# Clustered attention and two MLPs on one core: another order for the comparisons, the weight conversion and the output tiles

## The chip, the cores and the metric

One core of one Trainium2 chip runs the whole program. The metric is the device time of one execution in microseconds (us). TensorE is called PE here (PEld is its weight load), VectorE DVE, ScalarE ACT, GpSimd POOL, and SP is the engine that issues most of the DMAs. A number like L503 is a line of the kernel before.

## What is computed

The inputs q, k and v have the shape (2, 8, 768, 64) in float32; there are 16 centroids for each of the 8 heads. Every query and every key goes to its nearest centroid, and a query sees the keys of its own cluster only:

```python
q_assign = np.argmax(np.einsum('bhsd,hcd->bhsc', q_n, c_n), axis=-1)
k_assign = np.argmax(np.einsum('bhsd,hcd->bhsc', k_n, c_n), axis=-1)
mask = q_assign[:, :, :, None] == k_assign[:, :, None, :]
scores = np.where(mask, scale * q @ k.T, -1e9)
attn = exp(scores - max) / (sum + 1e-9);  x = attn @ v
```

The result, 1536 rows of 512, goes through two MLPs one after the other, each 512 → 2048 → 512. The first has g = h · cos h between its two products, the second g = h for h ≥ 1, 0 for h ≤ −1 and (h + 1)² / 4 between. The weights of both MLPs arrive as 64-bit floats.

## The kernel before, in words

**Attention.** The work is cut into 8 pairs (a batch entry and two heads), each with 4 units (a head, and one half of the queries): 32 units u. A unit has 6 slots k = 0 to 5. `run_slot` goes through all slots in order, and the order in which Python emits the instructions is the order of each engine's list: nothing is reordered behind it. Work for a later slot is queued by `later(n, f)` and emitted by `next_slot` n slots on.

In every slot, PE transposes a third of the unit's probabilities (`p_transpose`, L550), and ACT or, for k = 2 and 5, DVE copies them to SBUF (L555, L553). In slots 0, 2 and 5 PE also makes the scores of a tile of the next unit (L494, L497) into one of two PSUM buffers; DVE takes their row max (L503) and ACT the exp (L512), which frees the buffer. In slot 5 `p_v` (L564) multiplies with v, and ACT copies the output (`o_parts`, L575). PE's transposes all go through three PSUM buffers, `ps_t`, in turn, whoever uses them.

**The path to x.** Some slots after the exps DVE makes reciprocals of the row sums (L529) and POOL spreads them (`spread`, L536, tile rb). When both heads of a half are done, POOL moves rows together (`o_rows`, L584, L585), PE transposes rb into r and DVE multiplies (`finish`, L594, L596), and POOL splits the result into a high and a low part (`x_parts`, L601, L602: xh and xl, which the first MLP reads).

**Preparing a pair.** `prep_pair` is a generator, and `plan` says in which slot each of its eleven steps runs, and whether ahead of the unit's p_v (False) or behind everything else in the slot (True): four steps that transpose q and k (L332), the products with the centroids dt (L389) and their transposition pd (L396), the comparisons (L443 and L444 on DVE; L446 on POOL; L449; L451 on DVE), which end in one-hot rows (tile dots), and last the transposition of those (L468, tile po), the scaling on ACT (L470, oht) and eight copies by DMA (L477) into the stacked tiles st that the scores read. For pair i ≥ 2 the comparisons begin in slot 23 counted from the pair i − 2, the last slot of a unit, so one unit in four carries them: the units 3, 7, 11, 15, 19 and 23, six in all.

**Weight conversion.** The weights come in 32 chunks. `convert_chunk` has six steps, in turn: abs on ACT (L142); DVE L144; L146; L149; DVE L152 with the high part on POOL (L158) and the DMA of the next chunk; the low part on DVE (L161). A chunk's raw words and its working tile wx each have one buffer, so the six steps of a chunk follow each other. During the attention one step runs behind the last slot of each unit from the ninth on (`pump` and `CONVERT`, 24 steps); the others run in the MLPs.

**MLPs.** `hidden` makes four blocks h of 128 columns with 12 matmuls each (L724 to L726) into four PSUM buffers; `g_cosine` then runs on ACT (n, L697; sine and square, L699 and L700) and DVE (r, L698; g, L703), and `output` multiplies with the second weight. The first hidden block's matmuls are the first PE work behind the attention. A weight slot is written by the conversion and read by the matmuls.

**Pools.** All tiles of the attention, xt0, xt1, xt2 and rb among them, are in `apool`, which is given back behind the last unit; the MLP's pool `mpool`, with the tile n, takes the same bytes.

Of the kernel before, what the change touches and what calls it, by code (L numbers as in the profile page):

```python
# [31 lines left out]
def attention_moe_moe(  # L32
# [73 lines left out]
    def later(n, f, *args):  # L106
        due.setdefault(now[0] + n, []).append((f, args))
# [13 lines left out]

    w0pool = ctx.enter_context(tc.tile_pool(name="w0pool", bufs=1))
    wslot = []
    wchunks = []
# [68 lines left out]
    with ExitStack() as actx:  # L193
# [37 lines left out]
        def centroid_load():  # L231
            ct = ap.tile([P, HS], F32, tag="xt0", bufs=2, name="ct")[:, :P].rearrange(
                "p (r d) -> p r d", r=2)
            nc.scalar.dma_start(ct[:, 0], centroids.rearrange("h c d -> (h c) d"))
            return ct

        def centroid_setup(ct):
# [9 lines left out]
            for _ in range(2):  # L247
# [6 lines left out]
            nc.vector.reciprocal(ss[:, 3:4], ss[:, 2:3])  # L254
            cd = ap.tile([P, HS], F32, tag="xt1", bufs=2, name="cd")[:, :P].rearrange(
                "p (r d) -> p r d", r=2)
# [20 lines left out]
        def prep_pair(i):  # L277
# [84 lines left out]
            if i == 0:  # L362
                dcs = []
                for s in range(2):
                    dt = ps_t.tile([P, HS], F32, tag="t", name=f"dt0_{s}")
                    for hf in range(2):
                        g = hf * 2 * C
                        with tc.issue_after(ins(tr)):
                            nc.tensor.matmul(dt[g:g + 2 * C], cw, t32s[(s, hf)],
                                             start=True, stop=True, tile_position=(0, g))  # L370
                    dc = ap.tile([P, HJ, P], F32, tag=("oht", "xt2")[s], bufs=1 + s, name=f"dc0_{s}")
                    dc = dc[:4 * C]
                    if s == 0:
                        nc.vector.tensor_copy(dc.rearrange("p j n -> p (j n)"), dt[:4 * C])
                    else:
                        nc.scalar.activation(dc.rearrange("p j n -> p (j n)"), dt[:4 * C], AF.Copy)
                    dcs.append(dc)
# [154 lines left out]
        def spread(u, den):  # L532
            i, h, hf = units[u]
            if h == 0:
                rb[(i, hf)] = ap.tile([P, HJ, 2, D], F32, tag="rb", bufs=2, name=f"rb{i}_{hf}")
            nc.gpsimd.tensor_scalar(  # L536
                rb[(i, hf)][:, :, h], den[:, :, 1].unsqueeze(2).to_broadcast([P, HJ, D]),
                1.0, 0.0, ALU.mult, ALU.add)
# [28 lines left out]
        def o_parts(u):  # L567
# [4 lines left out]

            t = ap.tile([P, HS], F32, tag=f"xt{h}", bufs=2, name=f"xt{h}_{i}_{hf}")
            xt.setdefault((i, hf), []).append(t)
            nc.scalar.activation(t, o, AF.Copy)  # L575
            if h == 1:
                later(1 if i == len(pairs) - 1 else 3, o_rows, i, hf, main, other)

        def o_rows(i, hf, main, other):
            t0, t = xt[(i, hf)]  # L580
            t2 = ap.tile([P, HS], F32, tag="xt2", bufs=2, name=f"xt2_{i}_{hf}")
            xt[(i, hf)] = (t, t2)
            for dst, rows, src in ((t2, other, t0[main]), (t2, main, t[other]), (t, other, t0[other])):
                nc.gpsimd.tensor_scalar(dst[rows], src, 1.0, 0.0, ALU.mult, ALU.add)  # L584
            nc.gpsimd.tensor_tensor(t, t, t2, ALU.add)  # L585
            later(2 if i == len(pairs) - 1 else 4, finish, i, hf)

        def finish(i, hf):
# [7 lines left out]
            nc.vector.tensor_tensor(t2, t1, r, ALU.mult)  # L596
            later(1 if i == len(pairs) - 1 else 2, x_parts, hp, b * S + hf * HS, t2)

# [26 lines left out]

        def run_steps(slot, batch_done):
            for made in steps.pop((slot, batch_done), ()):
                next(made)

        plan(1, *((n, True) for n in (-6, -5, -4, -3, -2, -1, -1, 0, 1, 2, 3)))  # L630
        for i in range(2, len(pairs)):
            s0 = (i - 2) * PAIR
            plan(i, *((s0 + n, d) for n, d in (
                (5, True), (11, False), (11, True), (17, False), (17, True), (23, False),
                (23, True), (24, True), (26, True), (27, True), (29, False))))

        def run_slot(slot):
            u, k = divmod(slot, NJ)
            at_slots = (0, 2, 4) if u < 0 else (0, 2, 5)
            new = -1 <= u < len(units) - 1 and k in at_slots  # L640
            n = (u + 1) * HJ + at_slots.index(k) if new else None
# [4 lines left out]
            if new and k == 0:  # L646
                scores_of(n)
            if u >= 0:
                p_transpose(u, k)
            if new and k > 0:  # L650
                scores_of(n)
            run_steps(slot, False)
            if u >= 0 and k == NJ - 1:
                p_v(u)
            if new:
                row_max(n)
                if k == NJ - 1:
                    row_exp(n)
            elif -1 <= u < len(units) - 1 and k in [m + 1 for m in at_slots]:
                row_exp((u + 1) * HJ + at_slots.index(k - 1))  # L660
            if u >= 0 and k == NJ - 1:
                o_parts(u)
            next_slot()
            if slot == 47:
                issue_chunk(0)
            run_steps(slot, True)
            if slot in CONVERT:
                pump(1)

        CONVERT = [n * NJ + NJ - 1 for n in range(8, 32)]  # L670
        with tc.manual_schedule(engines={
# [142 lines left out]
```

## Time and profile before

| | |
|---|---|
| median of 3 runs | 800.97 us (800.7 to 803.86) |
| the profiled execution | 800.59 us, its span 798.5 us |
| busy share of the span | PE 97%, PEld 77%, DVE 71%, ACT 48%, POOL 34% |
| mean granted clock of PE | 0.995 of full speed |
| attention up to the first unit's p_v | 31.09 us |
| the stretch of units from there to 259.09 us | 228.00 us, PE busy for 220.65 |
| the last units and the first hidden block, to 283.24 us | 24.15 us, PE busy for 18.58 |
| the rest of both MLPs | 515.26 us, PE busy for 511.65 |

The span runs from the first to the last instruction; the time of an execution is some 2 us more. Busy is time in which an engine runs an instruction; the ends of matmuls are modelled, so a stretch is better measured from one start to another. In a timeline an idle time is noted behind the instruction that it precedes, with what ended it: `[1.92 <-PE r L594]` means that the engine stood for 1.92 us until PE had made r at L594.

### The profile page before, as it was taken

Reading aid. Unit: us, or ns where it says so; the run is one execution under the profiler, and the core shown is the slowest. Engines: PE = TensorE matmul, PEld = TensorE weight load, DVE = VectorE, ACT = ScalarE, POOL = GpSimd, SP = SyncE. Lnnn points to the kernel's source line nnn. Section 1 sums busy time; section 2 is a strip of 40 time slices with the busy share of each in tenths; the row PEclk is TensorE's granted clock in tenths of the full one; section 3 lists DMA queues with packets and bytes.
Section 4 is the critical chain, followed back from the end, with each engine's and each line's share of the span. In section 5 each row is a group of like instructions: output and inputs, shape, how many; then the busy total and the mean of one; then the engine's idle time right before and its main releaser. Section 6 shows DMA issues by size and latency. Waiting matters only on the chain.

```text
span 798.5 us, 10663 instructions
## 1 busy us (share of the span) xinstructions
PE 775.5 (97%) x3935; PEld 611.1 (77%) x3936; DVE 565.0 (71%) x809; ACT 384.1 (48%) x712; POOL 268.4 (34%) x398
## 2 busy tenths in 40 slices
PE   8899999999999889999999999999999999999998
PEld 4576776676677668888888888888888888888886
DVE  6565767666777498777887888788868887755552
ACT  6678777786787375443334344222444332222220
POOL 4346557666534632221221212342131222111110
PEclk9999999999999999999999999999999999999999
DMA  8755654755240212313112122111221311000012
GB/s 199 162 136 122 175 124 126 164 140 123 62 121 2 68 43 102 105 53 106 53 56 103 53 80 79 53 54 53 68 91 53 106 53 53 1 0 1 16 51 92
DMA packets 46387, 65.93 MB, mean 83 GB/s; under 512 B 27904, under 2 KB 30848, under 8 KB 46336
## 3 DMA queue, kind: packets, MB, share of 16 engines
q1 hardware_dynamic: 46192, 65.22, 28.8%
q8 instruction: 31, 0.51, 0.3%
q14 instruction: 20, 0.16, 0.1%
q10 hardware_dynamic: 144, 0.03, 0.0%
HBM read 43.02 MB, written 3.15 MB: 58 GB/s over the span
## 4 chain that ended last, share of the span: by engine, by line
PE 64%; POOL 1%; ACT 1%; DVE 0%; issue 0%; POOLq 0%
PE y L726 11%; PE y L724 11%; PE y L725 11%; PE h L724 10%; PE h L726 10%; PE h L725 10%; POOL xt L585 0%; POOL xh L601 0%; POOL xt L584 0%; ACT L699 0%; ACT r L699 0%; ACT n L697 0%; POOL xl L602 0%; DVE g L703 0%; DVE acc L763 0%; DVE xt L596 0%
## 5 line engine op out<-in xcount | busy, mean ns | idle before, releaser
L686 POOL TENSOR_SCALAR gh<-g 128x512 fp32r<-128x512 f32 x96 | 72.0, 750 | 276.6 <-DVE g L717 163.0
L724 PE MATMUL h<-xh,w 128*128 128x512 f32 x384 | 149.6, 390 | 3.4 <-DVE g L703 3.4
L725 PE MATMUL h<-xl,w 128*128 128x512 f32 x384 | 149.5, 389 | 0.0
L726 PE MATMUL h<-xh,w 128*128 128x512 f32 x384 | 149.5, 389 | 0.0
L503 DVE TENSOR_REDUCE nm<-s 128x1 f32<-128x768 f32 x96 | 91.6, 954 | 42.6 <-PE s L497 39.7
L512 ACT ACTIVATE p<-s,nm 128x768 f32<-128x768 f32 x96 | 86.8, 904 | 22.3 <-DVE nm L503 15.4
L713 ACT ACTIVATE p<-h,ones 128x512 f32<-128x512 f32 x48 | 33.1, 690 | 132.5 <-DVE m L712 132.1
L690 DVE TENSOR_TENSOR gl<-g,gh 128x512 fp32r<-128x512 f32 x96 | 73.6, 768 | 21.0 <-POOL gh L686 15.2
L724 PEld LDWEIGHTS h<-xh,w 128*128 128x128 f32 x384 | 72.1, 188 | 18.7 <-DVE g L703 3.8
L725 PEld LDWEIGHTS h<-xl,w 128*128 128x128 f32 x384 | 72.1, 188 | 14.9
L726 PEld LDWEIGHTS h<-xh,w 128*128 128x128 f32 x384 | 72.1, 188 | 14.9
L550 PE MATMUL pt<-ident,p 128*128 128x128 f32 x576 | 77.5, 275 | 4.4 <-DVE p_t L553 2.7
L142 ACT ACTIVATE wx<-wraw 128x1024 f32<-128x1024 f32 x32 | 36.3, 1135 | 86.5 <-DMA wraw<-in_moe_w_out_dram 39.0
L550 PEld LDWEIGHTS pt<-ident,p 128*128 128x128 f32 x576 | 66.9, 141 | 10.9 <-DVE p_t L553 4.6
L494 PE MATMUL s<-st,st 128*128 128x384 f32 x192 | 74.1, 386 | 0.8 <-ACT p L512 0.5
L724 PE MATMUL y<-gh,w 128*128 128x512 f32 x192 | 74.7, 389 | 0.0
L725 PE MATMUL y<-gl,w 128*128 128x512 f32 x192 | 74.7, 389 | 0.0
L726 PE MATMUL y<-gh,w 128*128 128x512 f32 x192 | 74.7, 389 | 0.0
L724 PE MATMUL y<-w,gh 128*128 128x512 f32 x192 | 74.7, 389 | 0.0
L725 PE MATMUL y<-w,gh 128*128 128x512 f32 x192 | 74.7, 389 | 0.0
L726 PE MATMUL y<-w,gl 128*128 128x512 f32 x192 | 74.7, 389 | 0.0
L763 DVE TENSOR_TENSOR acc<-y,acc 128x512 f32<-128x512 f32 x72 | 49.1, 684 | 33.9 <-PE y L726 33.9
(118 smaller groups left out, 1376.9 us busy)
## 6 DMA issues: line engine op xcount, KB each, us to landing
wraw<-in_moe_w_in_dram SPq DMA_DIRECT2D x16, 1024.0 KB, 5.1
wraw<-in_moe_w_out_dram SPq DMA_DIRECT2D x16, 1024.0 KB, 4.7
st<-t SPq DMA_DIRECT2D x24, 192.0 KB, 4.2
st<-th SPq DMA_DIRECT2D x9, 384.0 KB, 3.9
st<-tl SPq DMA_DIRECT2D x18, 192.0 KB, 4.1
st<-th SPq DMA_DIRECT2D x18, 192.0 KB, 4.2
nat<-in_q_dram SPq DMA_DIRECT2D x8, 384.0 KB, 4.9
nat<-in_k_dram SPq DMA_DIRECT2D x8, 384.0 KB, 5.1
```

The source lines that it names most:

```text
L142: nc.scalar.activation(x, high.bitcast(F32), AF.Abs)
L494: nc.tensor.matmul(s[:, step, :HS], qt[:, 0, cols], kt[:, 0, kc], start=True, stop=False)
L503: nc.vector.tensor_reduce(nm, s[:, :, :HS], AX.XY, ALU.max, negate=True)
L512: nc.scalar.activation(p, s[:, :, :HS], AF.Exp, bias=nm, accum_out=dens[u][:, jj, 0:1])
L550: nc.tensor.transpose(ps[:, jj * P:(jj + 1) * P], p[:, kt * P:(kt + 1) * P], ident)
L686: nc.gpsimd.tensor_scalar(hi, g, 1.0, 0.0, ALU.mult, ALU.add)
L690: nc.vector.tensor_tensor(lo, g, hi.bitcast(F32), ALU.subtract)
L713: nc.scalar.activation(r, ph, AF.Relu, bias=mone)
L724: nc.tensor.matmul(o, lh, rh, start=first, stop=False)
L725: nc.tensor.matmul(o, lh, rl, start=False, stop=False)
L726: nc.tensor.matmul(o, ll, rh, start=False, stop=last)
L763: nc.vector.tensor_tensor(a, po, a, ALU.add)
```

## The change

Five things change.

- The tiles xt0, xt1, xt2, rb, and those of the start that share their buffers, go to a pool of their own, `xpool`, opened early and never given back before the end.
- `plan` gets four places in a slot instead of two: ahead of the transposition, ahead of p_v, beside (behind the output's copy and ahead of `next_slot`, that is, ahead of what `later` queued) and behind. For pairs from the third on, L443 and L444 go from behind to beside in slot 23, L449 from behind to ahead of the row max in slot 26, L451 from slot 27 to slot 29 ahead of p_v, and the one-hot transposition L468 with what follows from ahead of p_v in slot 29 to behind it. The second pair's steps are planned later as well: dt from before the first unit's slots to its slot 0, the comparisons from there to slots 2 to 5, L468 to slot 6.
- The second exp of a unit moves from slot 3 to slot 4, behind the copy of that slot.
- The conversion starts with unit 15 and follows a pattern over four units: in each fourth unit (15, 19, ...) abs ahead of p_v and L144 beside; then L146; then L149 and L152 together; then L161. That is 26 steps up to the last unit.
- The counts of `later` change: `o_rows` 3 slots on for all but the last unit, `finish` always 4, `x_parts` always 1.

```diff
+    xpool = ctx.enter_context(tc.tile_pool(name="xpool", bufs=1))
...
-            ct = ap.tile([P, HS], F32, tag="xt0", bufs=2, name="ct")[:, :P].rearrange(
+            ct = xpool.tile([P, HS], F32, tag="xt0", bufs=2, name="ct")[:, :P].rearrange(
...
-                rb[(i, hf)] = ap.tile([P, HJ, 2, D], F32, tag="rb", bufs=2, name=f"rb{i}_{hf}")
+                rb[(i, hf)] = xpool.tile([P, HJ, 2, D], F32, tag="rb", bufs=2, name=f"rb{i}_{hf}")
...
-            t = ap.tile([P, HS], F32, tag=f"xt{h}", bufs=2, name=f"xt{h}_{i}_{hf}")
+            t = xpool.tile([P, HS], F32, tag=f"xt{h}", bufs=2, name=f"xt{h}_{i}_{hf}")
...
-                later(1 if i == len(pairs) - 1 else 3, o_rows, i, hf, main, other)
+                later(1 if u == len(units) - 1 else 3, o_rows, i, hf, main, other)
...
-            t2 = ap.tile([P, HS], F32, tag="xt2", bufs=2, name=f"xt2_{i}_{hf}")
+            t2 = xpool.tile([P, HS], F32, tag="xt2", bufs=2, name=f"xt2_{i}_{hf}")
...
-            later(2 if i == len(pairs) - 1 else 4, finish, i, hf)
+            later(4, finish, i, hf)
...
-            later(1 if i == len(pairs) - 1 else 2, x_parts, hp, b * S + hf * HS, t2)
+            later(1, x_parts, hp, b * S + hf * HS, t2)
...
-        plan(1, *((n, True) for n in (-6, -5, -4, -3, -2, -1, -1, 0, 1, 2, 3)))
+        AHEAD_OF_T, AHEAD_OF_V, BESIDE, BEHIND = range(4)
+        plan(1, (-6, BEHIND), (-5, BEHIND), (-4, BEHIND), (-3, BEHIND), (0, AHEAD_OF_T),
+             (2, BEHIND), (2, BEHIND), (3, BEHIND), (5, BESIDE), (5, BESIDE), (6, BEHIND))
         for i in range(2, len(pairs)):
             s0 = (i - 2) * PAIR
             plan(i, *((s0 + n, d) for n, d in (
-                (5, True), (11, False), (11, True), (17, False), (17, True), (23, False),
-                (23, True), (24, True), (26, True), (27, True), (29, False))))
+                (5, AHEAD_OF_V), (11, AHEAD_OF_V), (11, BEHIND), (17, AHEAD_OF_V), (17, BEHIND),
+                (23, AHEAD_OF_V), (23, BESIDE), (24, BEHIND), (26, AHEAD_OF_V),
+                (29, AHEAD_OF_V), (29, BEHIND))))
...
+            exp_slots = (1, 3, 5) if u < 0 else (1, 4)
...
+            run_steps(slot, AHEAD_OF_T)
             if u >= 0:
                 p_transpose(u, k)
             if new and k > 0:
                 scores_of(n)
-            run_steps(slot, False)
+            run_steps(slot, AHEAD_OF_V)
+            if u >= FIRST and k == NJ - 1 and u % 4 == 3:
+                pump(1)
             if u >= 0 and k == NJ - 1:
                 p_v(u)
...
-            elif -1 <= u < len(units) - 1 and k in [m + 1 for m in at_slots]:
-                row_exp((u + 1) * HJ + at_slots.index(k - 1))
+            elif -1 <= u < len(units) - 1 and k in exp_slots:
+                row_exp((u + 1) * HJ + exp_slots.index(k))
             if u >= 0 and k == NJ - 1:
                 o_parts(u)
+            run_steps(slot, BESIDE)
+            if u >= FIRST and k == NJ - 1:
+                pump((1, 2, 1, 1)[u % 4])
             next_slot()
             if slot == 47:
                 issue_chunk(0)
-            run_steps(slot, True)
-            if slot in CONVERT:
-                pump(1)
-
-        CONVERT = [n * NJ + NJ - 1 for n in range(8, 32)]
+            run_steps(slot, BEHIND)
+
+        FIRST = 15
```

DVE, around the end of unit 11, where the comparisons of the fifth pair (mx4, eq4, dots4) stand. s38 to s41 are tiles of scores and nm38 to nm41 their row maxima; p12_t2 and p12_t5 are copies of transposed probabilities; L596 multiplies with r. Before:

```order
L503 TENSOR_REDUCE nm38_1595<-s38_1579 128x1
L529 RECIPROCAL den11_1436<-den11_1436 128x3
L596 TENSOR_TENSOR xt2_2_0_1541<-xt1_2_0_1497,r2_0_1602 128x384
L443 TENSOR_REDUCE mx4_1607<-pd4_1584 128x24
L444 TENSOR_TENSOR eq4_1608<-pd4_1584,mx4_1607 128x384
L149 SCALAR_TENSOR_TENSOR wx0_1310<-wraw0_1185,wx0_1310 128x1024
L503 TENSOR_REDUCE nm39_1623<-s39_1612 128x1
L553 COPY p12_t2_1648<-pt12_2_1644 128x384
L503 TENSOR_REDUCE nm40_1655<-s40_1650 128x1
L449 TENSOR_REDUCE mx4_1607<-eq4_1608 128x24
L451 TENSOR_TENSOR dots4_1502<-eq4_1608,mx4_1607 128x384
L553 COPY p12_t5_1677<-pt12_5_1673 128x384
```

After:

```order
L504 TENSOR_REDUCE nm38_1594<-s38_1578 128x1
L444 TENSOR_REDUCE mx4_1600<-pd4_1583 128x24
L445 TENSOR_TENSOR eq4_1601<-pd4_1583,mx4_1600 128x384
L530 RECIPROCAL den11_1436<-den11_1436 128x3
L597 TENSOR_TENSOR xt2_2_0_1540<-xt1_2_0_1497,r2_0_1605 128x384
L504 TENSOR_REDUCE nm39_1621<-s39_1610 128x1
L554 COPY p12_t2_1646<-pt12_2_1642 128x384
L450 TENSOR_REDUCE mx4_1600<-eq4_1601 128x24
L504 TENSOR_REDUCE nm40_1654<-s40_1648 128x1
L554 COPY p12_t5_1674<-pt12_5_1670 128x384
L452 TENSOR_TENSOR dots4_1502<-eq4_1601,mx4_1600 128x384
L504 TENSOR_REDUCE nm41_1700<-s41_1676 128x1
```

L443 and L444 (L444 and L445 after) now stand ahead of the reciprocal and of L596; the conversion step L149 has left this place; L449 stands ahead of the row max nm40 and L451 behind the copy p12_t5, where before they stood one behind the other between the two.

POOL, the same place (rb2_1 is the spread of unit 11; xh and xl are the parts of x; the L584 rows move output rows together for the next half). Before:

```order
L536 TENSOR_SCALAR rb2_1_1426<-den11_1436 128x3x64
L446 TENSOR_TENSOR eq4_1608<-eq4_1608,desc_63 128x384
L584 TENSOR_SCALAR xt2_2_1_1637<-xt0_2_1_1396 64x384
L584 TENSOR_SCALAR xt2_2_1_1637<-xt1_2_1_1599 64x384
L584 TENSOR_SCALAR xt1_2_1_1599<-xt0_2_1_1396 64x384
L585 TENSOR_TENSOR xt1_2_1_1599<-xt1_2_1_1599,xt2_2_1_1637 128x384
L601 TENSOR_SCALAR xh_103<-xt2_2_0_1541 128x384
L602 TENSOR_TENSOR xl_104<-xt2_2_0_1541,xh_103 128x384
```

After:

```order
L537 TENSOR_SCALAR rb2_1_1426<-den11_1436 128x3x64
L602 TENSOR_SCALAR xh_103<-xt2_2_0_1540 128x384
L603 TENSOR_TENSOR xl_104<-xt2_2_0_1540,xh_103 128x384
L447 TENSOR_TENSOR eq4_1601<-eq4_1601,desc_63 128x384
L585 TENSOR_SCALAR xt2_2_1_1637<-xt0_2_1_1397 64x384
L585 TENSOR_SCALAR xt2_2_1_1637<-xt1_2_1_1598 64x384
L585 TENSOR_SCALAR xt1_2_1_1598<-xt0_2_1_1397 64x384
L586 TENSOR_TENSOR xt1_2_1_1598<-xt1_2_1_1598,xt2_2_1_1637 128x384
```

The parts of x for the first half, L601 and L602, stood behind the rows of the second half and now stand ahead of L446 (L447 after), which is ahead of those rows in both.

ACT, where the attention ends and the first MLP begins (p31_t3 and p31_t4 are copies for the last unit, wx4 is a chunk's abs, xt1_7_1 the last output's copy, n and r belong to the first hidden block), with the semaphores that each row waits for, named by the engine or DMA queue that sets them. Before:

```order
L555 ACTIVATE p31_t3_3519<-pt31_3_3515 128x384 [waits PE_49,Activation_49]
L555 ACTIVATE p31_t4_3525<-pt31_4_3521 128x384 [waits PE_49]
L142 ACTIVATE wx4_3776<-wraw4_3486 128x1024 [waits DMAHW0_49,DVE_49,Pool_49]
L575 ACTIVATE xt1_7_1_3540<-o31_3533 128x384 [waits PE_49]
L697 ACTIVATE n_0_0_0_0_3591<-h0_0_0_0_3578 128x512 [waits DMAHW2_49,DMAHW3_49,DMAHW1_49,DMAHW4_49,DVE_49,DMAHW5_49,PE_49,DMAHW6_49,Activation_49,Pool_49]
L697 ACTIVATE n_0_0_0_1_3613<-h0_0_0_1_3600 128x512 [waits PE_49]
L699 ACT_TABLE_LOAD
L699 ACTIVATE r_0_0_0_0_3592<-r_0_0_0_0_3592 128x512 [waits DVE_49]
```

After:

```order
L556 ACTIVATE p31_t3_3516<-pt31_3_3512 128x384 [waits PE_49,Activation_49]
L556 ACTIVATE p31_t4_3522<-pt31_4_3518 128x384 [waits PE_49]
L143 ACTIVATE wx4_3530<-wraw4_3406 128x1024 [waits DMAHW0_49,DVE_49]
L576 ACTIVATE xt1_7_1_3539<-o31_3532 128x384 [waits PE_49]
L706 ACTIVATE n_0_0_0_0_3597<-h0_0_0_0_3584 128x512 [waits DMAHW3_49,DMAHW2_49,DMAHW4_49,DMAHW1_49,DMAHW5_49,PE_49,DMAHW6_49,Activation_49,Pool_49]
L708 ACT_TABLE_LOAD
L708 ACTIVATE r_0_0_0_0_3598<-r_0_0_0_0_3598 128x512 [waits DVE_49]
L706 ACTIVATE n_0_0_0_1_3619<-h0_0_0_1_3606 128x512 [waits PE_49]
```

The first n (L697, L706 after) waited for DVE among the others and now doesn't; the sine of the first block now stands ahead of the second n.

## Rows read from the trace of the kernel before

**Rows 1.** The page, busy time, share of the span and number of instructions.
```profile
PE 775.5 (97%) x3935; PEld 611.1 (77%) x3936; DVE 565.0 (71%) x809; ACT 384.1 (48%) x712; POOL 268.4 (34%) x398
```

**Rows 2.** Windows: stretch, us, PE, PEld, DVE, ACT, POOL busy (instructions), clock, DMA share, GB/s.
```profile
28.88:32.29 3.41, 3.41 (x14) 2.30 (x14) 1.51 (x2) 1.05 (x3) 0.00 (x0) 0.50 0.00 0
53.82:62.18 8.36, 7.59 (x50) 5.35 (x49) 6.21 (x11) 5.70 (x14) 3.66 (x6) 1.00 0.11 24
114.35:123.75 9.40, 7.88 (x50) 5.34 (x49) 7.34 (x13) 5.45 (x13) 5.05 (x7) 1.00 0.34 89
131.35:138.35 7.00, 7.00 (x49) 5.41 (x48) 5.19 (x8) 5.85 (x15) 6.24 (x9) 1.00 0.52 165
145.86:154.73 8.87, 7.90 (x50) 5.34 (x49) 6.81 (x13) 5.45 (x13) 4.51 (x7) 1.00 0.43 110
176.58:186.01 9.43, 7.92 (x49) 5.34 (x48) 7.37 (x13) 5.44 (x13) 5.55 (x8) 0.99 0.78 205
186.01:195.09 9.08, 9.08 (x53) 6.25 (x52) 4.60 (x8) 6.62 (x14) 4.99 (x9) 0.82 0.67 148
283.24:798.50 515.26, 511.65 (x2256) 423.35 (x2256) 378.41 (x504) 183.17 (x285) 112.79 (x135) 1.00 0.17 60
```

**Rows 3.** Timeline of DVE: start, us, instruction, idle before; unit from 114.35, one later.
```profile
117.09 0.55 DVE L596 TENSOR_TENSOR xt<-xt,r 128x384 f32<-128x384 f32 x1 [1.92 <-PE r L594]
117.56 0.55 DVE L443 TENSOR_REDUCE mx<-pd 128x24 f32<-128x384 f32 x1
...
118.69 1.22 DVE L149 SCALAR_TENSOR_TENSOR wx<-wraw,wx 128x1024 int32<-128x1024 int32 x1
...
121.16 0.95 DVE L503 TENSOR_REDUCE nm<-s 128x1 f32<-128x768 f32 x1
...
134.74 0.96 DVE L503 TENSOR_REDUCE nm<-s 128x1 f32<-128x768 f32 x1 [1.45 <-PE s L497]
```

**Rows 4.** Timeline of PE, the two waits of the unit from 114.35.
```profile
121.29 0.55 PE L550 MATMUL pt<-ident,p 128*128 128x128 f32 x3 [0.78 <-DVE p_t L553]
...
123.30 0.52 PE L468 MATMUL po<-ident,dots 128*128 128x128 f32 x3 [0.42 <-DVE dots L451]
```

**Rows 5.** Timeline of PE, the start.
```profile
22.70 0.55 PE L396 MATMUL pd<-ident,dc 128*128 128x128 f32 x3 [0.58 <-ACT dc L392]
...
28.28 0.52 PE L468 MATMUL po<-ident,dots 128*128 128x128 f32 x3 [2.05 <-DVE dots L451]
```

**Rows 6.** Timeline of PE, the end of the attention and the first hidden block.
```profile
265.87 0.55 PE L594 MATMUL r<-ident,rb 128*128 128x128 f32 x3 [1.53 <-POOL rb L536]
...
270.87 0.55 PE L594 MATMUL r<-ident,rb 128*128 128x128 f32 x3 [0.64 <-POOL rb L536]
...
279.45 0.39 PE L726 MATMUL h<-xh,w 128*128 128x512 f32 x1
283.24 0.50 PE L724 MATMUL h<-xh,w 128*128 128x512 f32 x1 [3.41 <-DVE g L703]
```

**Rows 7.** Timeline of ACT, the same place.
```profile
278.40 1.09 ACT L697 ACTIVATE n<-h 128x512 int32<-128x512 f32 x2 [6.80 <-POOL xl L602]
```

**Rows 8.** Groups of instructions: count, busy us, mean ns of one, idle before and releaser.
```profile
L512 ACT ACTIVATE p<-s,nm 128x768 f32<-128x768 f32 x96 | 86.8, 904 | 22.3 <-DVE nm L503 15.4
...
L144 DVE TENSOR_SCALAR wx<-wx 128x1024 f32<-128x1024 f32 x32 | 22.9, 717 | 32.7 <-ACT wx L142 32.7
...
L602 POOL TENSOR_TENSOR xl<-xt,xh 128x384 fp32r<-128x384 f32 x16 | 17.1, 1066 | 1.3
...
L601 POOL TENSOR_SCALAR xh<-xt 128x384 fp32r<-128x384 f32 x16 | 9.5, 591 | 2.5 <-DVE xt L596 2.5
```

**Rows 9.** Timeline of POOL: L446 in units 3 and 11.
```profile
58.39 1.01 POOL L446 TENSOR_TENSOR eq<-eq,desc 128x384 f32<-128x384 f32 x1 [2.47 <-DVE eq L444]
...
118.92 1.84 POOL L446 TENSOR_TENSOR eq<-eq,desc 128x384 f32<-128x384 f32 x1 [2.04 <-DVE eq L444]
```

**Rows 10.** Waits, by waiting instruction and releaser: us in all, count, longest.
```profile
POOL w L158 <- PE y L726: 4.2, 1, 4.2
```

More of the change, by code (lines that the diff above doesn't have):

```diff
@@ L254, in centroid_setup @@
             nc.vector.reciprocal(ss[:, 3:4], ss[:, 2:3])
-            cd = ap.tile([P, HS], F32, tag="xt1", bufs=2, name="cd")[:, :P].rearrange(
+            cd = xpool.tile([P, HS], F32, tag="xt1", bufs=2, name="cd")[:, :P].rearrange(
                 "p (r d) -> p r d", r=2)
@@ L370, in prep_pair @@
                                              start=True, stop=True, tile_position=(0, g))
-                    dc = ap.tile([P, HJ, P], F32, tag=("oht", "xt2")[s], bufs=1 + s, name=f"dc0_{s}")
+                    dc = (ap, xpool)[s].tile([P, HJ, P], F32, tag=("oht", "xt2")[s], bufs=1 + s, name=f"dc0_{s}")
                     dc = dc[:4 * C]
@@ L624, in plan, with run_steps @@
                 steps.setdefault(place, []).append(made)
-        def run_steps(slot, batch_done):
-            for made in steps.pop((slot, batch_done), ()):
+        def run_steps(slot, place):
+            for made in steps.pop((slot, place), ()):
                 next(made)
-        plan(1, *((n, True) for n in (-6, -5, -4, -3, -2, -1, -1, 0, 1, 2, 3)))
+        AHEAD_OF_T, AHEAD_OF_V, BESIDE, BEHIND = range(4)
+        plan(1, (-6, BEHIND), (-5, BEHIND), (-4, BEHIND), (-3, BEHIND), (0, AHEAD_OF_T),
+             (2, BEHIND), (2, BEHIND), (3, BEHIND), (5, BESIDE), (5, BESIDE), (6, BEHIND))
         for i in range(2, len(pairs)):
```

## The prediction

> **What bounds the kernel now.** I read the page first, then the trace stage by stage: windows, the timelines of PE, DVE and POOL around each idle stretch of PE, and the waits. The page's busy line shows PE busy for 775.5 us of the span [rows 1], and no other engine above 71%, so what counts is what PE waits for and how slowly it runs. Where PE can still gain is told by the windows [rows 2]. From 283.24 us to the end PE runs the two MLPs and waits for nothing: no gain is to be had there, and a loss only if a weight comes late. Everything to gain lies ahead of that, in three places.
>
> First, one unit in four. A unit is the stretch from one p_v (L564) to the next. The unit from 131.35 us, which carries a transposition of the next pair, takes 7.00 us with PE never idle. The units that carry the comparisons of a pair take more: 8.36 us from 53.82 (and once more for the next pair), 9.40 from 114.35 (and again from 209.59), 8.87 and 9.43 [rows 2]. Above 7.00 these six are 1.36, 1.36, 2.40, 1.87, 2.43 and 2.40: **11.8 us**. What happens in one is seen in the unit from 114.35. On DVE, L596 stands first and waits 1.92 us for r, which PE makes only behind p_v; the comparisons stand behind it, then a conversion step of 1.22 us, and only then the row max of the scores [rows 3]. Everything on DVE is late from there, so the copy that frees a PSUM buffer for the next transposes is late (PE waits 0.78 us) and so is L451, for which the one-hot transposes L468 wait 0.42 us [rows 4].
>
> Second, the start: PE waits 0.58 us for dc and 2.05 us for L451 of pair 1 [rows 5], and directly behind that the granted clock stands at 0.50, its lower level of 1.2 GHz, for 3.41 us [rows 2], which costs 1.7. The same happens once more behind the unit from 176.58, one of the six: the unit after it has a mean clock of 0.82 over 9.08 us, that is 18% lost, 1.6 us [rows 2].
>
> Third, the tail. PE waits 1.53 and 0.64 us for reciprocals spread by POOL, and 3.41 us for g of the first hidden block [rows 6]. The last goes back to ACT: its n (L697) waits 6.80 us for the last x_parts (L602) [rows 7], because tile n lies in bytes that the attention's pool gives back only when its last reader is through.
>
> **The change, part by part.** The profiled execution took 800.59 us around a span of 798.5; the median is 800.97, 0.4 more. I sum against 800.59.
>
> *Start.* dt, pd and the comparisons of pair 1 go behind the first scores and transposes of the batch, and L468 behind p_v. The waits of 0.58 and 2.05 lose their place; with no stall before it, the clock has no reason in these rows to fall: 2.63 + 1.7 = 4.3. Late next are the scores: they now follow each other directly, and the third needs the buffer that the first exp frees. Price: one exp, 0.90 us [rows 8]. I take **−3.4**; bounds −0.8 (the drop of the clock stays and two exps are waited for) and −4.3.
>
> *The six units.* L443 and L444 move ahead of the reciprocal and L596, to the time in which DVE waited 1.92 us. They cost nothing there: DVE idles, and the two take 118.69 − 117.56 = 1.13 us [rows 3]. L149 leaves these units, but in the last three of them L144, 0.72 us, now stands with the comparisons [rows 8]: 1.92 − 1.13 − 0.72 leaves 0.07, so it just fits, if ACT has its abs ready. L449 goes ahead of a row max, L451 to just ahead of p_v, L468 and the eight copies of L477 behind it. The copies fill SP's queue later than before, but are read first by scores three units on, some 21 us by 7.00 us a unit [rows 2]: nothing. x_parts moves ahead of L446 on POOL, 0.59 + 1.07 us [rows 8]. L446 then starts about 1.7 us behind L596's end; with L596 at 117.1 as now, near 119.4, for 1.01 us [rows 9]; L449 can follow at 120.5 and the row max that stands behind it at 121.0, against 121.16 now [rows 3]. So the row max is hardly earlier, but the copy ahead of it is, and p_v no longer has L468 before it. I let half a microsecond per unit stand for what remains there, and for the copy of L468's result, which now holds a PSUM buffer into the next unit: 6 × 0.5 = 3.0. With the clock's 1.6: 11.8 + 1.6 − 3.0 = **−10.4**; bounds −2.5 (rival 1) and −13.4.
>
> L446's duration decides here. It took 1.01 us in the unit with no conversion beside it and 1.84 beside L149 [rows 3, 9]. The Trainium skill, "SBUF — State Buffer", section "SBUF: two separate sides", has VectorE and GpSimd share a port pair that an instruction of VectorE with two SBUF inputs holds for its whole length, so that GpSimd is blocked, not slowed. By that rule 1.01 holds in the changed kernel, where DVE stands waiting or reads PSUM. I take 1.01 because no conversion step stands beside L446 in the new order of DVE; if it is 1.84 all the same, the sum is about 5 us worse (6 × 0.83).
>
> How much the units are worth depends on the view as well. Busy time alone says 9.40 − 7.88 = 1.52 us for the unit from 114.35, its length says 2.40 [rows 2]. I go by lengths, which are from start to start; the 50 rows of matmuls of the 8.36 us unit hold 7.59 us against 7.00 for 49, so busy time contains some of the waiting. "Perfetto Trace Analysis" of the Trainium skill, section "Identifying the Most-Contended Engine", likewise calls matmul busy time a poor measure of how near PE is to its limit. By busy time alone the whole kernel could gain no more than 798.5 − 775.5 = 23.0 us [rows 1].
>
> *Conversion.* 26 steps instead of 24 run in the attention, begun seven units later. Of the pattern only L149 and L152 back to back, 2.4 us on DVE, can hurt, in four units. In the unit from 131.35 DVE stands idle 1.45 us ahead of a row max, though a step already lies in the same stretch; a second step of 1.22 fits [rows 3]. I take **+0.5**; bounds 0 and 4.8, four times the step if its cover is gone. The exp behind a copy changes the order of two ACT instructions whose results are wanted a unit later: nothing.
>
> *Tail.* xt, rb and their kin lie in a pool that is never given back. n then waits no more for x_parts, only for POOL's last spread, ACT's copies and PE. h of the first block ends with its twelfth matmul, right behind the r that starts at 270.87; the fifth block wants the same buffer 36 matmuls later, behind 279.45: some 8 us. From n to the stalled matmul took 283.24 − 278.40 = 4.84 [rows 6, 7]: it fits. Late next is r of the last unit: it stands directly behind p_v and waits for abs, reciprocal and spread. finish at 4 slots for all puts r 7_0 behind that p_v too, so 1.53 and 0.64 have p_v as cover. 1.53 + 0.64 + 3.41 = 5.6; less 0.2 for the last spread: **−5.4**; bounds −3.4 (the two small waits stay) and −5.6.
>
> Sum: −3.4 − 10.4 + 0.5 − 5.4 = −18.7, 781.9 for an execution like the profiled one, **782.3 us** as a median.
>
> **Rivals.**
> 1. *L446 becomes the new wait.* Behind x_parts it ends too late, DVE stands at L449 and with it the row max, and the six units keep most of their surplus. For it: POOL needs 1.7 us more before L446, and L449 now stands ahead of a row max instead of behind one. Against it: r, not the comparisons, sets L596's start, so L446 is no later than r makes it. Middle −2.5 instead of −10.4: 790.2.
> 2. *All six units become clean,* no clock drops, no exp waits, no conversion cost: −4.3 − 13.4 − 5.6 = −23.3, 777.7. For it: DVE is busy 71% only. Against it: the chain on DVE worked out above leaves little slack.
> 3. *The last spread inherits the tail's wait,* since ACT does abs of a chunk and DVE its L144 ahead of the reciprocal; 2.2 us (1.53 + 0.64) remain: 784.5.
> 4. *Slower:* chunks converted two steps earlier overwrite a weight slot that PE still reads. The row shows one such wait of 4.2 us at L158 [rows 10], today hidden by slack. With some twelve chunks moved, 4.2 each and no cover, +50: 832. It decides from 1.6 us a chunk, where it eats 18.7. Against it: two steps are small beside the slot's time in use, and PE in the MLPs shows no wait for a weight.
> 5. *Nothing happens,* the stalls only change their names: 797 to 805.
>
> **How the numbers follow.** Forecast 0.55 (its own range 779 to 787), rival 1 0.17, rival 2 0.18, rival 3 0.05, rival 4 0.03, rival 5 0.02. The range reaches from rival 2 less 1.2 us (units that I call clean and that aren't quite, seen the other way) to rival 1: 776.5 to 790.5; it leaves out rivals 4 and 5 and the outer halves of 1 and 2. A measurement of this kernel can tell about 0.5%, 4 us, from no change. Rivals 1 to 3 and the forecast lie beyond it, so faster has 0.95 less a little for their tails: 0.94; same 0.03; slower 0.03.
>
> **What would show it right or wrong.** Right: the six units at 7.0 to 7.9 us; DVE's comparisons ahead of L596; L446 at 1.0 us; no half clock behind the start and in the unit after the fifth of the six; PE's first matmul of the fifth hidden block without a wait. Rival 1 would show as idle time of DVE at L449, released by POOL L446; rival 3 as r waiting for rb; rival 4 as waits for w in the MLPs. My prediction would be wrong if a unit not among the six grew, above all those with L149 and L152 together, or if scores waited for exp all along the batch rather than at the start alone.

## The result and the profile after

The changed kernel takes 777.19 us (median of 4 runs, 776.94 to 777.49) against 800.84 us of the kernel before beside it (800.66 to 803.86): a ratio of 0.9696, 95% interval 0.9673 to 0.972. The profiled execution took 776.98 us, 23.6 less than the 800.59 of the one before. The forecast was 782.3, so the gain is 5 us larger than expected; of the outcomes described, rival 2 (all units clean, 777.7) is the nearest.

The page's line of busy time and the windows of the changed kernel (stretch, us, PE, PEld, DVE, ACT, POOL busy, clock, DMA share, GB/s) answer to [rows 1, 2]:

```profile
PE 766.1 (99%) x3936; PEld 610.0 (79%) x3936; DVE 566.8 (73%) x809; ACT 380.1 (49%) x712; POOL 263.5 (34%) x398
```

```profile
27.27:240.85 213.58, 213.31 (x1460) 160.21 (x1459) 159.41 (x241) 168.38 (x370) 125.59 (x199) 1.00 0.55 133
49.08:56.08 7.00, 7.00 (x50) 5.41 (x49) 4.85 (x8) 4.41 (x11) 3.57 (x6) 1.00 0.62 153
107.08:114.08 7.00, 7.00 (x50) 5.42 (x49) 4.94 (x9) 4.33 (x11) 3.92 (x7) 1.00 0.50 123
114.08:121.58 7.50, 7.50 (x53) 5.73 (x53) 5.80 (x11) 6.48 (x14) 5.55 (x9) 1.00 0.76 167
136.08:143.08 7.00, 7.00 (x50) 5.42 (x49) 5.54 (x10) 5.26 (x12) 4.01 (x7) 1.00 0.41 113
172.09:179.58 7.49, 7.49 (x52) 5.72 (x52) 6.57 (x12) 6.47 (x14) 2.59 (x5) 1.00 0.76 167
240.85:259.78 18.93, 18.34 (x97) 13.14 (x97) 11.47 (x16) 9.84 (x18) 12.46 (x17) 1.00 0.26 90
259.78:774.90 515.12, 511.52 (x2257) 423.24 (x2255) 378.32 (x504) 183.20 (x286) 111.91 (x135) 1.00 0.17 60
```

The units with comparisons, 8.36 to 9.43 us before, take 7.00 (the last 6.66), and PE is never idle in them. Its busy time fell as well, from 775.5 to 766.1 us for the same matmuls, so busy time did contain some of the waiting. By stages, each measured from one start to another:

| stage | before | after | change | forecast |
|---|---|---|---|---|
| to the first p_v | 31.09 | 27.27 | −3.8 | −3.4 |
| from there to p_v of the last unit but one | 228.00 | 213.58 | −14.4 | −10.4 + 0.5 |
| from there to the fifth hidden block | 24.15 | 18.93 | −5.2 | −5.4 |
| the rest of the MLPs | 515.26 | 515.12 | −0.1 | 0 |

DVE in the unit from 107.08 of the changed kernel (start, us, instruction, idle before) answers to [rows 3]:

```profile
107.73 0.55 DVE L444 TENSOR_REDUCE mx<-pd 128x24 f32<-128x384 f32 x1
108.39 0.56 DVE L445 TENSOR_TENSOR eq<-pd,mx 128x384 f32<-128x384 f32 x1
...
109.82 0.56 DVE L597 TENSOR_TENSOR xt<-xt,r 128x384 f32<-128x384 f32 x1 [0.79 <-PE r L595]
110.46 0.96 DVE L504 TENSOR_REDUCE nm<-s 128x1 f32<-128x768 f32 x1
111.52 0.56 DVE L554 COPY p_t<-pt 128x384 f32<-128x384 f32 x1
113.06 0.55 DVE L450 TENSOR_REDUCE mx<-eq 128x24 f32<-128x384 f32 x1 [0.99 <-POOL eq L447]
113.53 0.95 DVE L504 TENSOR_REDUCE nm<-s 128x1 f32<-128x768 f32 x1
114.39 0.55 DVE L554 COPY p_t<-pt 128x384 f32<-128x384 f32 x1
```

The comparisons run in the wait for r, of which 0.79 us is left. The row max behind them starts 110.46 − 107.08 = 3.4 us into the unit, where it started 119.82 − 114.35 = 5.5 us into it before. DVE does stand at L450 for POOL, as rival 1 had it, for 0.99 us. What PE reads is in time all the same: the copy L554 behind it starts 7.3 us behind the unit's start, 8.7 before. The two rows of the kernel before:

```profile
119.82 0.95 DVE L503 TENSOR_REDUCE nm<-s 128x1 f32<-128x768 f32 x1
...
123.07 0.55 DVE L553 COPY p_t<-pt 128x384 f32<-128x384 f32 x1
```

PE's waits in the changed kernel (waiting line, releaser, us in all, times, longest); the rows left out, and one of the two waits for the exp, lie in the first 20 us:

```profile
PE s L495 <- ACT p L513: 1.1, 2, 0.7
...
PE r L595 <- POOL rb L537: 0.6, 1, 0.6
...
PE pt L551 <- ACT oht L471: 0.3, 1, 0.3
PE pt L551 <- ACT p_t L556: 0.3, 1, 0.3
```

Behind the first 20 us there is no wait for g, for one-hot rows or for DVE's copies any more.

### The profile page after: what moved, and what is told of

It reads as the page before. It is cut to its first block, busy times and chain, and to the rows that moved or that the text cites. A ratio compares the mean times of both kernels' runs of the same rounds, so it can differ in the third digit from the quotient of the medians.

```text
span 774.9 us, 10689 instructions
## 1 busy us (share of the span) xinstructions
PE 766.1 (99%) x3936; PEld 610.0 (79%) x3936; DVE 566.8 (73%) x809; ACT 380.1 (49%) x712; POOL 263.5 (34%) x398
## 4 chain that ended last, share of the span: by engine, by line
PE 97%; DMA 1%; ACT 1%; DVE 1%; issue 0%; POOL 0%; POOLq 0%; ACTq 0%
PE y L733 11%; PE h L734 11%; PE y L735 11%; PE h L735 11%; PE y L734 11%; PE h L733 11%; PE pt L551 8%; PE o L565 8%; PE s L495 5%; PE s L498 4%; PE ptq L333 1%; PE r L595 1%; PE dt L390 1%; DMA nat<-in_q_dram 1%; DMA st<-th 0%; PE pd L397 0%
## 5 line engine op out<-in xcount | busy, mean ns | idle before, releaser
L551 PE MATMUL pt<-ident,p 128*128 128x128 f32 x576 | 75.4, 274 | 0.5 <-ACT oht L471 0.3
```

The costliest lines, as they stand in the source:

```text
L551: nc.tensor.transpose(ps[:, jj * P:(jj + 1) * P], p[:, kt * P:(kt + 1) * P], ident)
```

## The experiments

The runs e1 to e7, e9 and e10 start from the changed kernel, e8, c1 and c2 from the kernel before. The kernel before took between 799.02 and 803.82 us beside them, at mean granted clocks between 0.998 and 0.991 (see the last section), and the runs are of more than one chip; so parts are compared by stages and units of the profiled execution. The start is not alike to the tenth of a microsecond: in the runs that leave it as the change has it, the first p_v begins between 27.18 and 27.73. Lengths of units in us, those with comparisons (3, 7, 11, 15, 19, 23) and the ones behind each:

| run | six units | units behind them |
|---|---|---|
| before | 8.36 8.36 9.40 8.87 9.43 9.40 | 7.33 7.46 7.60 7.33 9.08 7.28 |
| changed | 7.00 five times, 6.66 | 7.49 or 7.50 five times, 7.52 |
| e1, old conversion | 7.00 7.00 7.70 7.16 7.69 7.35 | 7.49 8.19 8.28 7.76 8.38 7.72 |
| e2, comparisons behind | 7.68 7.69 7.69 7.61 7.61 7.27 | 7.34 five times, 7.00 |
| e3, one-hot rows early | 8.04 three times, 8.05 twice, 7.71 | 7.00 to 7.02, 6.68 |
| e6, x_parts later | 7.00 five times, 6.66 | 7.33 five times, 7.00 |
| e7, old exp | 7.00 five times, 6.66 | 7.89 or 7.90 |
| c1, before + conversion | 8.37 8.36 8.37 8.29 8.29 8.28 | 7.33 or 7.34, 6.68 |
| c2, before + plan | 7.00 7.00 7.85 7.32 7.84 7.50 | 7.33 7.67 7.61 7.33 7.64 7.28 |

**e1: the old conversion schedule put back.**

```diff
-            if u >= FIRST and k == NJ - 1:
-                pump((1, 2, 1, 1)[u % 4])
...
+            if slot in CONVERT:
+                pump(1)
```

> The changed kernel with the old conversion schedule alone put back: one step behind the last slot of each unit from unit 8 on. In units 11, 19 and 23 a step of 1.2 us then stands behind the multiplication with r and ahead of the row max again. Theory (the units have slack on DVE now, about half of the step is hidden): the units 11, 19, 23 take 7.5 us instead of 7.0, unit 15 some 7.2, the sum +2, 779. Rival A (the comparisons alone made the six units long, the conversion is free): no change, 777.2. Rival B (the step costs what the units with it had above those without, 9.40 - 8.36): +1.0 in three units and +0.5 in one, 780.7.

Measured: 783.87 us, 0.9778 (0.9751 to 0.9804). All three expectations were too low. The units 11, 19 and 23 grow by 0.7 as the theory had it, but the units behind the six, 8 to 24, grow by 0.2 to 0.9 as well: in this run they hold a step beside the one-hot transposes, which the change has moved there. The stretch of units is 5.3 us longer and the MLPs behind the fifth hidden block 1.5. DVE and POOL of this run:

```profile
111.44 1.22 DVE L150 SCALAR_TENSOR_TENSOR wx<-wraw,wx 128x1024 int32<-128x1024 int32 x1
112.58 0.95 DVE L504 TENSOR_REDUCE nm<-s 128x1 f32<-128x768 f32 x1
...
119.14 1.82 DVE L153 SCALAR_TENSOR_TENSOR wx<-wraw,wx 128x1024 int32<-128x1024 int32 x1
```

```profile
111.61 1.42 POOL L602 TENSOR_SCALAR xh<-xt 128x384 fp32r<-128x384 f32 x1 [0.84 <-DVE xt L597]
...
118.27 0.51 POOL L305 TENSOR_SCALAR t<-t 128x384 fp32r<-128x384 f32 x1
118.86 1.01 POOL L306 TENSOR_TENSOR t<-t,t 128x384 fp32r<-128x384 f32 x1
```

The step costs twice: it stands 1.2 us ahead of the row max, which starts 1.61 us behind L597 (0.64 in the changed kernel), and xh beside it takes 1.42 us where it takes 0.51 everywhere in the changed kernel's attention. In the next unit it is DVE's step that is long, 1.82, beside POOL's L306.

**e2: the two comparisons behind the multiplication again.**

```diff
-                (23, AHEAD_OF_V), (23, BESIDE), (24, BEHIND), (26, AHEAD_OF_V),
+                (23, AHEAD_OF_V), (23, BEHIND), (24, BEHIND), (26, AHEAD_OF_V),
```

> The changed kernel with the two comparisons on DVE alone put back behind the reciprocal and the multiplication with r, in the same slot. The row max of the next scores then starts 1.13 us later in all six units. Theory (slack takes half of it): the six units take 7.5 us, +3, 780.2. Rival A (the comparisons' place is what made the six units 1.36 us too long): +8, 785. Rival B (it was the conversion step beside them): no change, 777.2.

Measured: 779.33 us, 0.9722 (0.9696 to 0.9749). The six units grow by 0.6 to 0.7, the ones behind get 0.16 shorter (0.5 the last): +2.6 over the units, the theory's size. Rival A (the place alone made 1.36 each) and rival B fall.

**e3: one-hot rows ahead of p_v again.**

```diff
-                (23, AHEAD_OF_V), (23, BESIDE), (24, BEHIND), (26, AHEAD_OF_V),
-                (29, AHEAD_OF_V), (29, BEHIND))))
+                (23, AHEAD_OF_V), (23, BESIDE), (24, BEHIND), (26, BEHIND),
+                (27, BEHIND), (29, AHEAD_OF_V))))
```

> The changed kernel with the second half of the comparisons alone put back: the reduction behind the row max in slot 26, the equality in slot 27, and the one-hot transposes ahead of p_v in slot 29. Theory: with the first half early, the one-hot rows are ready about 0.3 us after PE wants them, so PE waits 0.3 us in six units, +1.8, 779. Rival (the one-hot rows' place was the larger part of the 0.78 + 0.42 us of waits): +1.0 in each of the six, 783.

Measured: 780.09 us, 0.9732 (0.97 to 0.9763). The six grow by 1.04, the units behind shrink by 0.5, since the transposes change units: +3.0 over the units, between the theory's 1.8 and the rival's 6: each of the six grew as the rival had it, but half of that came back one unit later. PE and DVE of this run:

```profile
115.86 0.52 PE L469 MATMUL po<-ident,dots 128*128 128x128 f32 x3 [0.53 <-ACT p L513]
```

```profile
114.57 0.55 DVE L450 TENSOR_REDUCE mx<-eq 128x24 f32<-128x384 f32 x1
115.15 0.56 DVE L452 TENSOR_TENSOR dots<-eq,mx 128x384 f32<-128x384 f32 x1
```

PE waits 0.53 us, not 0.3. The releaser named is an exp; the one-hot rows of L452 end at the same time, 115.7, and are what the transposes read. So even early comparisons don't serve transposes ahead of p_v.

**e4 and e8: the pool of its own, taken from the changed kernel and given to the one before.**

```diff
-            t = xpool.tile([P, HS], F32, tag=f"xt{h}", bufs=2, name=f"xt{h}_{i}_{hf}")
+            t = ap.tile([P, HS], F32, tag=f"xt{h}", bufs=2, name=f"xt{h}_{i}_{hf}")
```

(e4; the other tiles of `xpool` likewise, and e8 the other way round.)

> The changed kernel without the pool of its own: xt, rb and their kin lie in the attention's pool again. The first n then waits for the last part of x, which POOL ends at 255.95, instead of starting at 251.94. Theory (g of the first block is held back on DVE anyway, by a conversion step that waits for POOL behind the parts of x, and comes only 0.36 us before PE wants the buffer): PE waits some 0.7 us, 777.9. Rival (the pool is what took away the wait of 3.41 us): 780.6.

> The kernel before with the pool of its own alone added. n of the first hidden block can start at 271.7 instead of 278.40. Theory (what the prediction said: this wait is the 3.41 us): PE's wait for g goes, 797.4. Rival (DVE's conversion steps behind POOL's parts of x take its place, as in the changed kernel): g comes little earlier, -0.5 to -2, 799 to 800.

Measured: e4 778.09 us, 0.9706 (0.968 to 0.9732); its last stage takes 19.55 instead of 18.93 us, +0.6, as the theory had it. e8 796.56 us, 0.9938 (0.9915 to 0.996); the last stage takes 20.58 instead of 24.15, −3.6, but 0.8 of it comes back in the MLPs, with a wait of 0.6 for a later g: nearer the theory than the rival. (Its profiled execution has no fall of the clock behind unit 19, 1.6 us that the pool did not bring.) In e4 the first n does wait again, for more than before:

```profile
256.40 0.60 ACT L705 ACTIVATE n<-h 128x512 int32<-128x512 f32 x1 [7.79 <-POOL xl L602]
```

yet PE loses 0.45 us to it. The pool takes away 3.6 us alone and 0.6 beside the other edits: its gain and theirs are largely the same time.

**e5: the old plan of the second pair.**

```diff
-        plan(1, (-6, BEHIND), (-5, BEHIND), (-4, BEHIND), (-3, BEHIND), (0, AHEAD_OF_T),
-             (2, BEHIND), (2, BEHIND), (3, BEHIND), (5, BESIDE), (5, BESIDE), (6, BEHIND))
+        plan(1, *((n, BEHIND) for n in (-6, -5, -4, -3, -2, -1, -1, 0, 1, 2, 3)))
```

> The changed kernel with the old plan of the second pair alone put back (products, comparisons and one-hot transposes ahead of the first p_v). Theory (the start's gain is this plan's alone): PE waits some 0.6 and 2.0 us again, the first p_v starts at 31.1 instead of 27.27, and the clock stands at its lower level for 3.4 us behind the stall: +3.8, 781.0. Rival (the second exp's new place or the other counts made the start faster): +2 or less, and no fall of the clock.

Measured: 780.61 us, 0.9739 (0.9707 to 0.977). The first p_v starts at 30.77, the unit behind it is 0.5 shorter: +3.0. The waits are back, the fall of the clock isn't (PE, then a window whose clock is the third number from the end):

```profile
23.05 0.55 PE L397 MATMUL pd<-ident,dc 128*128 128x128 f32 x3 [0.58 <-ACT dc L393]
28.62 0.52 PE L469 MATMUL po<-ident,dots 128*128 128x128 f32 x3 [2.06 <-DVE dots L452]
```

```profile
28.00:31.50 3.50, 2.88 (x22) 2.34 (x24) 1.99 (x4) 2.31 (x5) 0.00 (x0) 1.00 0.00 0
```

The start's gain is the plan's. The fall of the clock did not come in the profiled execution (779.95 us, mean clock 1.000) nor in one more (779.96); the other two took 781.26 and 781.59 at 0.998. So the expectation's part on the clock holds at most for some executions.

**e6: x_parts one slot later again.**

```diff
-            later(1, x_parts, hp, b * S + hf * HS, t2)
+            later(1 if i == len(pairs) - 1 else 2, x_parts, hp, b * S + hf * HS, t2)
```

> The changed kernel with the parts of x 2 slots behind the multiplication again, as before (1 for the last pair). POOL then does the product with desc ahead of the parts of x, about 1.6 us earlier, and DVE's wait of 0.99 us for it in each of the six units goes. Theory (that wait of DVE holds nothing that PE wants): no change, 777.2. Rival (it still costs PE something): -0.5 to -2, 775 to 776.7.

Measured: **775.79 us**, 0.9674 (0.9649 to 0.9699), the fastest kernel of the study: its runs (775.56 to 775.94) lie below all of the changed kernel's. The theory is wrong, the rival right: the units behind the six fall to 7.33, the last of them to 7.00, 1.4 us over the units. POOL, DVE and ACT of this run, the same place as above:

```profile
109.29 1.01 POOL L447 TENSOR_TENSOR eq<-eq,desc 128x384 f32<-128x384 f32 x1
```

```profile
111.69 0.54 DVE L450 TENSOR_REDUCE mx<-eq 128x24 f32<-128x384 f32 x1
112.16 0.95 DVE L504 TENSOR_REDUCE nm<-s 128x1 f32<-128x768 f32 x1
```

```profile
113.14 0.90 ACT L513 ACTIVATE p<-s,nm 128x768 f32<-128x768 f32 x1
```

The unit starts at 106.79 here. L447 starts 2.5 us into it (5.0 in the changed kernel), DVE doesn't wait, and the exp behind the row max starts 6.35 us into it (7.43: there at 114.51). What follows on ACT is earlier too, down to L471, the copy of the transposed one-hot rows, which holds one of the PSUM buffers of the transposes. In the changed kernel PE's weight load waits for that copy in each of the six units behind (first row, unit 12; second, all waits), in unit 24 until PE itself is idle for 0.27 us; in this run no row waits for it:

```profile
118.36 0.31 PEld L551 LDWEIGHTS pt<-ident,p 128*128 128x128 f32 x3 [0.18 <-ACT oht L471]
```

```profile
PEld pt L551 <- ACT oht L471: 1.4, 6, 0.5
```

**e7: the second exp ahead of the copy again.**

```diff
-            exp_slots = (1, 3, 5) if u < 0 else (1, 4)
+            exp_slots = (1, 3, 5) if u < 0 else (1, 3)
```

> The changed kernel with the second exp in slot 3 again, ahead of the copy p_t4. Theory: in the six units the row max it waits for ends at 114.39 in unit 11, so the copy p_t4 moves behind it, from 113.4 to 115.8, and p_v, which reads it from about 115.5, waits 0.3 to 0.8 us; the other units are not touched: +3, 780. Rival A: nothing hangs on it, 777.2. Rival B: all 31 units grow by 0.2, +6, 783.

Measured: 779.75 us, 0.9725 (0.97 to 0.975); +2.7 over the units, as the theory had it: p_v waits for the copy p_t4, and 0.4 us falls on each of the units behind the six, and 0.38 on unit 2, which the theory did not expect. In c2, where x_parts stood as before, the old place of the exp cost nothing of the kind (units 4 and 16: 7.33). So the new place of the exp mends what the new place of x_parts brings; the two together weren't undone in one run on the changed kernel.

**e9 and e10: the last pair.**

```diff
-            later(4, finish, i, hf)
+            later(2 if i == len(pairs) - 1 else 4, finish, i, hf)
```

(e9, `o_rows` likewise; e10 is e6 without the steps of unit 31.)

> The changed kernel with the old counts for the last pair alone put back (rows 1 slot on for both halves, the multiplication with r 2 slots on). Theory (behind p_v the spreads are covered): PE's waits of 1.53 and 0.64 us for POOL's spread come back in place of the 0.58 us of the changed kernel, +1.6 in the stretch from the last unit but one to the fifth hidden block, 778.8. Rival (the same wait, only elsewhere): no change, 777.2.

> The changed kernel with the parts of x 2 slots behind the multiplication (1 for the last pair), and no conversion steps in the last unit. Theory: the first part gives 1.3 to 1.4 as in its own run (775.8); without abs and the step behind it, the last reciprocal and spread come before PE wants r, and the wait of 0.58 us goes: 775.2. Rival (the two steps that now fall into the first MLP delay its g, which had only 0.36 us to spare): 776 or more, with a wait for g.

Measured: e9 778.65 us, 0.9703 (0.9687 to 0.9719), the last stage 20.33 us, +1.4: waits of 1.39 and 0.33 in place of 0.58. e10 776.35 us, 0.9674 (0.9656 to 0.9693), 0.6 behind e6 in the last stage: neither expectation. The steps did not go to the MLP; the chunk's abs stands ahead of two copies on ACT instead, DVE's L147 and L150 run beside the spread, and that takes 1.20 us instead of 0.70, so that r waits 1.17:

```profile
247.09 1.20 POOL L537 TENSOR_SCALAR rb<-den 128x192 f32<-128x192 f32 x1
```

**c1 and c2: conversion and plan alone, on the kernel before.**

> The kernel before with the new conversion pattern alone. Theory (the pattern is worth the most by itself: it takes the step away from the row max and POOL's work): the units 11, 15, 19 and 23 fall to 8.36 us, those of units 3 and 7, the sum -4.5, 796.5. Rival A (the pattern helps only where the comparisons have moved too): -1 or less, 800. Rival B (it gives all that its undoing cost, 7): 794.

> The kernel before with the new places of the preparation of the third to the last pair alone (comparisons early, one-hot rows behind p_v; old conversion, counts, pools, exps and second pair). Theory (from the units of the run with the old conversion, and 0.4 more per pair for the exp ahead of a copy): the six units take 7.0 to 7.7 us, the units behind them 7.9 to 8.8, the sum -5, 796. Rival A (the comparisons' place carries the whole gain of the middle): -12, 789. Rival B (without the other parts it only moves the stall into the next unit): 0 to -2, 800.

Measured: c1 791.29 us, 0.9859 (0.9841 to 0.9876); c2 792.68 us, 0.9867 (0.9839 to 0.9895). By the table, the pattern alone brings all six units to what the ones without a step had, 8.3 to 8.4, and the units behind to 7.34; 3.9 us in the six and 1.0 in five of the units behind (without the one of 9.08). That is the theory's size; the span of the profiled execution is 9.0 shorter in all, mostly since its last stage is 2.2 shorter and the clock doesn't fall behind unit 19 (1.6). The plan alone brings the six down by 9.3, between the theory and rival A, and leaves the ones behind nearly as they were (+0.2 in the same five). The profiled execution of c2 took 788.8 us at a mean clock of 1.000, the other three 792.56 to 793.05 at 0.993, so the 11.8 us by which its span is shorter hold what the clock did as well. Each falls short in the units where the other's work still stands.

## Why the prediction was right or wrong

**Start, −3.4: near, and in part by a term that comes and goes.** Measured −3.8, and another 0.5 in unit 0, where the rest of the fall of the clock lay. In e5 and c2, with the old plan and no fall, unit 0 ends at 37.49 and 37.55 us, against 38.82 before and 34.47 after: some 3.0 are the plan's, 1.3 the clock's in this execution, for which the prediction had 1.7. The price of an exp, 0.90, was near: of the two waits for it, 0.47 and 0.66, the first stands in the kernel before too.

**The six units: the mechanism right, the size wrong, and this is the step that failed.** The prediction let "half a microsecond per unit stand for what remains there", 6 × 0.5 = 3.0. Nothing remains in the six: they take 7.00. What remains lies in the units behind: 37.51 us for five of them against 37.00 before (without the one of 9.08), +0.5. The prediction's own sign of being wrong, a unit outside the six that grows, is there in this small size: 7.33 to 7.50 in units 4 and 16, 7.28 to 7.52 in unit 24. Why it was mis-sized: the residual stood for two things. The chain on DVE was right to 0.2 us (the row max at 121.0 forecast is 6.65 us into the unit, measured 113.53 − 107.08 = 6.45), but no instruction of PE waits for that row max in the unit, and none was named. The copy of L468's result, which was named, is what PE's weight loads do wait for, 1.4 us over six units (e6), where half a microsecond in each was put down for both. The others that make up the 4.5 us between −9.9 and −14.4: 0.5 for the conversion, which was no cost; 0.9 in the first three units, of which 0.5 in unit 0 goes with the start and 0.38 in unit 2 is the second exp's place, which the prediction priced at nothing (e7 gives it back); 0.3 in unit 23, which is 6.66; and 0.3 elsewhere.

**L446 at 1.01 us: right,** 1.00 in all six units (1.84 before beside L149, [rows 9]). Either edit alone does that: it takes 1.00 to 1.02 in c1 and in c2, and 1.00 in e1, where the step falls on xh instead. The Trainium skill, "SBUF — State Buffer", section "SBUF: two separate sides", has the loser of the shared port pair blocked until the other is through: e1 agrees on both sides, xh at 1.42 instead of 0.51 beside L150, and L153 at 1.82 instead of 1.22 beside L306. Waiting for the other's end, xh would take 112.66 − 111.61 + 0.51 = 1.56 and L153 119.87 − 119.14 + 1.22 = 1.95, both 0.13 to 0.14 more than measured.

**Rival 1: wrong in its place, right in its mechanism.** L446 behind x_parts does hold DVE, but costs 1.4 us in all (e6), in the units behind, where 7.9 were priced.

**Conversion, +0.5: too much.** L149 and L152 together fit: the units 17, 21, 25 and 29 take what they took before, to 0.05 us. What the pattern brings, the prediction had in the six units' term only; undone beside the other edits it costs 5.3 us in the units and 1.5 in the MLPs (e1).

**Tail, −5.4: right in its sum,** −5.2. The three waits are gone, and rival 3's exists, as 0.58 us. But the prediction gave each wait to one edit, and there the runs differ: the pool brings 3.6 alone and 0.6 beside the others (e8, e4), the last pair's counts 1.4 beside them (e9), and the conversion pattern, which the tail's sum left out, 2.2 alone (c1). Which part of the 5.2 is whose has no single answer.

**Rival 4 (a weight slot still read): nothing of it,** the MLPs take 515.1 us against 515.3.

## What to carry to other kernels

A helper's work belongs where its engine waits anyway, ahead of the instruction that it waits for; and a long step that nobody waits for must not stand behind that instruction, ahead of one that the bound engine needs. Before a residual is put into a sum, name the instruction of the bound engine that will wait for it, and price that wait alone: here the part with such an instruction was real, the part without one was nothing. Parts that remove the same wait don't add: undo each from the finished kernel as well as trying it alone, since here that also found an edit (x_parts earlier) that cost 1.4 us and hid among gains.

## What the runs showed of the hardware that was not expected

The fall of the granted clock to 0.50, half of the 2.4 GHz, doesn't follow every stall. In the profiled execution of the kernel before it stood behind the waits at 28.28 and in unit 19 [rows 2]; e5 has the same wait of 2.06 us with the clock at 1.00 right behind it, and in e8 the unit behind the stalled unit 19 runs at full clock:

```profile
186.00:193.27 7.27, 7.27 (x51) 5.58 (x49) 4.44 (x8) 6.53 (x14) 3.26 (x7) 1.00 0.80 175
```

It is all the same a matter of the kernels with such stalls, as the mean clocks of all executions show:

| kernel | executions | mean clock | us |
|---|---|---|---|
| before, beside the experiments | 22 | 0.991 to 0.998 | 803.82 to 799.02 |
| e8 (old start) | 5 | 0.995 to 0.998 | 798.26 to 796.03 |
| c1 (old start) | 3 | 0.998 | 791.26 to 791.73 |
| c1 (old start) | 1 | 1.000 | 790.14 |
| c2 (old start) | 3 | 0.993 | 792.56 to 793.05 |
| c2 (old start) | 1 | 1.000 | 788.8 |
| e5 (old start) | 2 | 0.998 | 781.26, 781.59 |
| e5 (old start) | 2 | 1.000 | 779.95, 779.96 |
| the nine with the new start | 36 | 0.999 or 1.000 | each within 0.7 of its kernel's others |

(The nine are the changed kernel, e1 to e4, e6, e7, e9 and e10.) So the 3.3 us of the 23.6 that are the clock's (1.7 and 1.6, by the prediction's reading) are a gain of the change, of a size that differs from execution to execution of the kernel before. What decides in which execution the clock falls stays open.
